# First chunk's first-layer up-products in two float32r parts, with a fourth buffer for converted weights

## The chip, the cores and the metric

The kernel runs on one core of one Trainium2 chip. The metric is the device time of one execution in microseconds (us); less is better. The engines are TensorE (PE: matrix products; PEld is its weight loads), VectorE (DVE), ScalarE (ACT), GpSimd (POOL) and SyncE (SP, which here only issues DMAs).

## The reference

Three layers follow each other in float32: attention that keeps the 32 largest scores of each row, and two pairs of dense products with 1152 tokens, width 512 and inner width 2048.

```python
def _attn_ref(q, k, v):                      # (2, 8, 576, 64) each
    scores = scale * np.matmul(q, k.transpose(0, 1, 3, 2))
    kth = np.partition(scores, -top_k, axis=-1)[..., -top_k:-top_k + 1]
    scores = np.where(scores >= kth, scores, -1000000000.0)
    scores = scores - np.max(scores, axis=-1, keepdims=True)
    attn = np.exp(scores)
    attn = attn / (np.sum(attn, axis=-1, keepdims=True) + 1e-09)
    return np.matmul(attn, v)

def _moe_ref(x, w_in, w_out):                # first layer
    h = x @ w_in
    return (np.maximum(h, 0.0) + np.log1p(np.exp(-np.abs(h)))) @ w_out

def _moe2_ref(x, w_in, w_out, alpha):        # second layer
    h = x @ w_in
    return (np.maximum(h, 0.0) + alpha * np.minimum(h, 0.0)) @ w_out
```

The weights reach the chip as float64 bit patterns; the kernel converts them to float32 itself.

## The kernel before

**Tiles and chunks.** The 1152 tokens are nine tiles of 128, in three chunks: tiles 3 and 4 (chunk 0), tiles 5, 6, 7 (chunk 1), tiles 8, 0, 1, 2 (chunk 2). A chunk's attention has to be done before its first layer, that before its second. The attention of the next chunk runs beside the layers of the one before.

**Attention.** A tile has eight heads, here called rows; row 76 is tile 7, head 6. For each row PE makes the scores (`pss`, L444), ACT copies them (`s`), DVE finds the 32 largest with four MAX8 and three MATCH_REPLACE8 (`m`, `r`, L453 and L456), a mask is built on ACT (L490) or DVE (L492), POOL subtracts it (`e`, L495), ACT takes the exponential and its sum (L497), PE transposes (`pp`, `pq`) and multiplies with the values (`pav`, L540). When a tile's eight rows are done, `finish` spreads the reciprocal sums with PE (`pr`), ACT copies that (`xn`), and DVE multiplies it with `pav`. With one part that product is the layer's input `xh`; with two parts it is `xn` (L598), from which ACT casts `xh` (L599) and POOL or DVE subtracts to get `xl`.

**Layers.** A layer has 16 steps j. `up(j)` is four products of 128 x 128 weights with n columns (n is 256, 384, 512 in chunks 0, 1, 2) into `ph`; ACT and DVE make `g` of it; `down(j)` multiplies `g` into the accumulators `pa`. In `NATIVE` layers the products are whole float32 (L637 for up, L685 for down), which the profile records as two matmuls each. In the others, `three` (L607 to L609) makes three float32r products of a high and a low part. The names carry layer and chunk: `ph00`, `pa00` first layer of chunk 0, `ph10`, `pa10` its second layer, `ph01` first layer of chunk 1. Before the change both layers of chunk 0 are `NATIVE`.

**Weights.** `convert` brings a float64 unit from memory (`cr`), makes the float32 unit `cx` with two DVE operations (L328, L333), one of ACT (L335, 2.5 us) and four of POOL (L339), and stores it as `ws`. There are 32 units; the first 24 are converted ahead, the last 8 when chunk 0's second layer first uses them, straight from `cx`. `fetch` loads a stored unit into a ring of four (`w`); where the layer is not native, `divide` splits it there: a cast on ACT (L357) and two subtractions of 512 columns on POOL (L351) or DVE (L352).

**Order.** Each engine runs its instructions in the order in which they stand. That order is made at build time by `Planner`: operations with lengths and due times, taken one after another by engine. The due times come from the tables at the head of the kernel (`T0`, `PACE`, `ROWS_DUE`, `AHEAD` and others). SP alone issues all DMAs.

## Time and profile before

| | us |
|---|---|
| median of 3 runs (684.16 to 687.32) | 685.82 |
| the profiled execution | 685.44 |
| its span | 683.7 |
| PE busy | 620.0 (91%) |
| DVE busy | 544.3 (80%) |
| ACT busy | 489.1 (72%) |
| POOL busy | 354.0 (52%) |

The profile's page gives busy time over the whole span, and the span in 40 slices of 17.1 us with the busy share of each in tenths. Stages are told apart by the first product of each: in this execution `ph00` starts at 133.7 us, `ph10` at 219.6, `ph01` at 296.2 (296.5 in the chain), the second layer of chunk 1 at 406.3, chunk 2 at 496.3. Matmul durations in the timeline contain the pipeline's depth; what one costs in a dense row of them is the distance of their starts, which the chain of waits prints as their length.

### The profile page before, as it was taken

The page shows a single profiled execution, that of the slowest core. Times are in us where ns is not written, and L with a number is a line of the kernel's source. Part 1 is how long each engine was busy: PE and PEld are TensorE (multiplying, and loading weights), DVE is VectorE, ACT ScalarE, POOL GpSimd, SP SyncE. Part 2 cuts the span into 40 slices and gives each one's busy share as a digit, 9 for nine tenths or more (in the row PEclk, how much of TensorE's full clock was granted, in tenths as well). Part 3 has the DMA queues.
Part 4 walks back from the last instruction along what each step waited for, and adds up shares of the span by engine and source line. Part 5 has one row for each costly group of instructions (what it writes and reads, how often), then busy time and mean ns, then how long its engine had stood idle before and what let it go on. Part 6 is the DMA issues. An engine that isn't in the chain of part 4 may idle for free.

```text
span 683.7 us, 10246 instructions
## 1 busy us (share of the span) xinstructions
PE 620.0 (91%) x3432; PEld 462.6 (68%) x3432; DVE 544.3 (80%) x1028; ACT 489.1 (72%) x981; POOL 354.0 (52%) x386
## 2 busy tenths in 40 slices
PE   5556545699999999999999999999999999999997
PEld 3334423466666666568788778788888888788885
DVE  5999999999999998999989899989654544544442
ACT  4877867798889778988889888777676555534431
POOL 0776665656564579657878768688310112121120
PEclk9566755699999999999999999999999999999999
DMA  8767865677787766732332122113243231313121
GB/s 332 255 244 232 261 210 208 203 289 244 293 268 262 277 225 209 246 128 88 121 112 77 66 89 93 63 63 124 77 154 107 80 123 63 123 62 123 62 93 62
DMA packets 28276, 109.59 MB, mean 160 GB/s; under 512 B 3264, under 2 KB 3264, under 8 KB 24128
## 3 DMA queue, kind: packets, MB, share of 16 engines
q1 hardware_dynamic: 28224, 108.94, 46.2%
q8 instruction: 27, 0.44, 0.3%
q14 instruction: 25, 0.20, 0.1%
HBM read 89.79 MB, written 19.14 MB: 159 GB/s over the span
## 4 chain that ended last, share of the span: by engine, by line
PE 76%; DVE 14%; ACT 3%; DMA 2%; issue 2%; POOL 1%; SPq 0%; DVEq 0%; POOLq 0%
PE ph L607 8%; PE pa L607 8%; PE pa L685 8%; PE ph L637 8%; PE ph L609 8%; PE ph L608 8%; PE pa L609 8%; PE pa L608 8%; DVE m L453 6%; DVE r L456 5%; PE pss L444 5%; PE pp L511 4%; DMA cr<-in_w_dram 2%; DVE cr L333 2%; DVE cx L328 2%
## 5 line engine op out<-in xcount | busy, mean ns | idle before, releaser
L453 DVE MAX8 m<-r 128x8 f32<-128x576 f32 x216 | 156.1, 746 | 0.2
L495 POOL TENSOR_TENSOR e<-s,e 128x288 f32<-128x288 f32 x144 | 124.1, 877 | 59.2 <-ACT e L490 40.2
L339 POOL TENSOR_TENSOR cx<-cx,cr 128x256 int32<-128x256 int32 x128 | 96.6, 780 | 74.6 <-ACT cr L335 64.0
L351 POOL TENSOR_TENSOR w<-w 128x512 fp32r<-128x512 f32 x66 | 90.2, 1378 | 72.9 <-ACT w L357 66.4
L456 DVE MATCH_REPLACE8 r<-m,r 128x576 f32<-128x576 f32 x144 | 106.3, 740 | 0.0
L351 POOL TENSOR_TENSOR gl<-g,gh 128x384 fp32r<-128x384 f32 (+1 forms) x38 | 44.2, 1162 | 104.3 <-ACT gh L665 104.1
L335 ACT ACTIVATE cr<-cr 128x1024 int16<-128x1024 uint32 x32 | 80.1, 2503 | 12.5 <-DVE cr L333 12.3
L444 PE MATMUL pss<-ks,q 64*128 64x288 f32 x320 | 75.5, 538 | 14.5 <-ACT s L449 6.2
L511 PE MATMUL pp<-ident,e 128*128 128x128 f32 x288 | 48.5, 302 | 39.2 <-ACT e L497 28.8
L511 PEld LDWEIGHTS pp<-ident,e 128*128 128x128 f32 x288 | 36.8, 154 | 57.9 <-ACT e L497 35.6
L357 ACT CAST w<-w 128x1024 fp32r<-128x1024 f32 x64 | 66.9, 1045 | 8.8 <-DMA w<-ws 8.8
L607 PE MATMUL pa<-w,gh 128*128 128x512 f32 x160 | 65.7, 410 | 0.0
L444 PEld LDWEIGHTS pss<-ks,q 64*128 64x128 f32 x320 | 34.7, 224 | 44.7 <-issue 11.9
L352 DVE TENSOR_TENSOR w<-w 128x512 fp32r<-128x512 f32 x62 | 48.0, 809 | 20.7 <-ACT w L357 20.6
L608 PE MATMUL pa<-w,gl 128*128 128x512 f32 x160 | 63.3, 396 | 0.0
L609 PE MATMUL pa<-w,gh 128*128 128x512 f32 x160 | 63.2, 395 | 0.0
L449 ACT COPY s<-pss 128x288 f32<-128x288 f32 x144 | 51.9, 406 | 14.1 <-PE pss L444 13.7
L453 DVE MAX8 m<-s 128x8 f32<-128x576 f32 x72 | 53.4, 746 | 10.4 <-ACT s L449 10.3
L652 DVE SCALAR_TENSOR_TENSOR g<-ph,g 128x256 f32<-128x256 f32 (+2 forms) x48 | 26.5, 552 | 41.4 <-ACT g L651 38.3
L497 ACT ACTIVATE e<-e,nb 128x576 f32<-128x576 f32 x72 | 55.7, 775 | 5.0 <-POOL e L495 5.0
L656 ACT ACTIVATE g<-ph 128x256 f32<-128x256 f32 (+2 forms) x48 | 23.8, 495 | 44.3 <-PE ph L609 37.9
L658 DVE SCALAR_TENSOR_TENSOR g<-g,rest,ph 128x256 f32<-128x256 f32 (+2 forms) x48 | 29.3, 611 | 31.8 <-ACT g L656 30.8
(127 smaller groups left out, 1417.4 us busy)
## 6 DMA issues: line engine op xcount, KB each, us to landing
w<-ws SPq DMA_DIRECT2D x88, 512.0 KB, 3.2
cr<-in_w_dram SPq DMA_DIRECT2D x32, 1024.0 KB, 6.9
ws<-cx SPq DMA_DIRECT2D x32, 512.0 KB, 7.6
v<-in_v_dram SPq DMA_DIRECT2D x12, 320.0 KB, 8.5
ks<-in_k_dram SPq DMA_DIRECT2D x12, 288.0 KB, 5.5
q<-in_q_dram SPq DMA_DIRECT2D x10, 256.0 KB, 6.0
out_dram<-o SPq DMA_DIRECT2D x9, 256.0 KB, 2.0
al<-in_alpha_dram SPq DMA_DIRECT2D x1, 8.0 KB, 9.0
```

What stands on the lines that cost most here:

```text
L335: op("ACT", ACT_LOW, due, lambda: nc.scalar.activation(raw().bitcast(I16)[:, :, 2], low(), AF.Copy, scale=2.0 ** -29), reads=[f], writes=[ ...
L339: op("POOL", on_pool(cs.stop - cs.start), due, lambda cs=cs: nc.gpsimd.tensor_add(f().bitcast(I32)[:, cs], f().bitcast(I32)[:, cs], high() ...
L351: lambda cs=cs: nc.gpsimd.tensor_sub(lo()[:, cs], x()[:, cs], hi()[:, cs].bitcast(F32)),
L357: op("ACT", on_act(WIDE), due, lambda: nc.scalar.copy(w()[:, 0, :], x()), reads=reads, writes=[w])
L444: nc.tensor.matmul(pss[n](), qr()[n * D:(n + 1) * D, pair, :], ks()[n * D:(n + 1) * D, cs], start=j == 0, stop=j == len(qk) - 1)
L453: op("DVE", on_dve(n), due, lambda: nc.vector.max(out=out(), in_=x()), reads=reads, writes=writes)
L456: op("DVE", on_dve(n) + 0.067, due, lambda: nc.vector.match_replace(out=out(), in_to_replace=found(), in_values=x(), imm_value=LOWEST), re ...
L495: op("POOL", on_pool(HS), due - AHEAD["mask"][ci], lambda cs=cs: nc.gpsimd.tensor_sub(e()[:, cs], s()[:, cs], e()[:, cs]), reads=[s], writ ...
L511: nc.tensor.transpose(pp()[:, c * P:(c + 1) * P], e()[:, c0 + c * P:c0 + (c + 1) * P], ident)
L607: nc.tensor.matmul(acc, ah, b_l, start=first, stop=False)
L608: nc.tensor.matmul(acc, a_l, bh, start=False, stop=False)
L609: nc.tensor.matmul(acc, ah, bh, start=False, stop=last)
```

## The change

The entries of `NATIVE` now name the part of a layer: `up` and `down` of chunk 0's second layer and `down` of its first layer stay whole float32, the first layer's `up` does not. So chunk 0's input has a high and a low part, the eight first-layer up units are divided in the ring, and the up-products go through `three` with 256 columns. The input's buffers are named by the chunk's parity in place of two in turn. `CXB`, the buffers for converted units, goes from 3 to 4. The planner's tables have new numbers throughout (a line or two shown), and the last six rows of each chunk get a due time of their own (`TAIL`). Code below moves down by one or two lines.

```diff
-MASK_SPARE = [134483.1, 915.2, -1585.2]
-CXB = 3
+MASK_SPARE = [1237.6, 843.7, -1292.2]
+CXB = 4
...
-PACE = [1522.8, 891.5, 6605.4, 9176.3, 2106.0, 687.1]
+PACE = [1786.6, 161.6, 6140.8, 8035.3, 911.5, 7716.3]
...
-NATIVE = {(1, 0), (0, 0)}
+TAIL = 6
+NATIVE = {(1, 0, 'down'), (0, 0, 'down'), (1, 0, 'up')}
...
-        return a + (b - a) * (i - first_row[ci]) / (first_row[ci + 1] - first_row[ci])
+        due = a + (b - a) * (i - first_row[ci]) / (first_row[ci + 1] - first_row[ci])
+        return due - AHEAD["tail"][ci] * (i >= first_row[ci + 1] - TAIL)
...
-    def features(name, bufs, ci, layer):
+    def features(name, ci, layer):
+        tag = name + str(ci % 2) * (not layer)
         n = sum(len(CHUNKS[c]) for c in (among[ci] if layer else [ci])) * P
-        if (layer, ci) in NATIVE:
-            return (buf(name + "h", bufs, [P, KT, n], F32, f"{name}h{ci}"),)
-        return tuple(buf(name + g, bufs, [P, KT, n], F32R, f"{name}{g}{ci}") for g in "hl")
+        if (layer, ci, "up") in NATIVE:
+            return (buf(tag + "h", 1, [P, KT, n], F32, f"{name}h{ci}"),)
+        return tuple(buf(tag + g, 1, [P, KT, n], F32R, f"{name}{g}{ci}") for g in "hl")
...
-            self.native = (layer, ci) in NATIVE
-            self.passes = 4 if self.native else 3
+            self.native = {part: (layer, ci, part) in NATIVE for part in ("up", "down")}
+            self.passes = {part: 4 if native else 3 for part, native in self.native.items()}
...
-                        if self.native:
+                        if self.native["up"]:
                             nc.tensor.matmul(hp(), whole_of(w)[:, cs], self.x[c][0]()[:, c, :],
...
-                        fetch((layer, (j + ULEAD) // GROUP, 0), no, ci, moe_due(ci, layer, j + ULEAD), lay.native)
+                        fetch((layer, (j + ULEAD) // GROUP, 0), no, ci, moe_due(ci, layer, j + ULEAD), lay.native["up"])
```

Three places of the new order follow; numbers behind a name tell buffers apart.

On PE, where the first layer of chunk 0 begins. `pp50`, `pp51`, `pq51` are transposes of tile 5's rows, `pr4` belongs to tile 4's finish. Before:

```order
L511 MATMUL pp50_1093<-ident_64,e0_71 128x128 x4
L587 MATMUL pr4__1103<-ident_64,rs4_961 64x128 x8
L511 MATMUL pp51_1116<-ident_64,e0_71 128x128 x4
L517 MATMUL pq51_1127<-ident_64,e0_71 128x128
L637 MATMUL ph00_0_1133<-xh0_628,w0_287 128x256 x4
L444 MATMUL pss560_1150<-ks13_620,q5_0_696 128x288
```

After:

```order
L589 MATMUL pr4__1104<-ident_64,rs4_1000 64x128 x8
L512 MATMUL pp51_1118<-ident_64,e0_71 128x128 x4
L518 MATMUL pq51_1134<-ident_64,e0_71 128x128
L445 MATMUL pss560_1139<-ks13_583,q5_0_691 128x288
L445 MATMUL pss570_1141<-ks13_583,q5_0_691 128x288
L541 MATMUL pav5__1147<-pt0_73,v10_139 64x128 x10
L445 MATMUL pss561_1179<-ks13_583,q5_0_691 128x288
L445 MATMUL pss571_1181<-ks13_583,q5_0_691 128x288
L609 MATMUL ph00_0_1189<-xl0_737,w0_287 128x256
L610 MATMUL ph00_0_1189<-xh0_712,w0_287 128x256
L611 MATMUL ph00_0_1189<-xh0_712,w0_287 128x256
```

Four score products and one value group of tile 5 now stand ahead of the first up-product, and where one whole product stood there are three.

On DVE, at the last MAX8 of tile 7 (row 76), the last tile of chunk 1; `cx107`, `cx116` are converted units, `g10_12` a step of chunk 0's second layer. Before:

```order
L453 MAX m77_2337<-r77_2353 128x8
L456 MATCH_REPLACE r76_2347<-m76_2325,r76_2347 128x576
L328 TENSOR_SCALAR cx107_2460<-cr107_2399 128x1024
L453 MAX m76_2325<-r76_2347 128x8
L333 TENSOR_SCALAR cr107_2399<-cr107_2399 128x1024
```

After:

```order
L454 MAX m81_2612<-s81_2536 128x8
L457 MATCH_REPLACE r76_2544<-m76_2470,r76_2544 128x576
L660 SCALAR_TENSOR_TENSOR g10_12_2614<-g10_12_2614,rest_70,ph10_12_2582 128x256
L329 TENSOR_SCALAR cx116_2631<-cr116_2570 128x1024
L454 MAX m76_2470<-r76_2544 128x8
```

One more unit is converted ahead of tile 7's last MAX8 than before, and the first MAX8 of rows 80 and 81 (chunk 2) both stand ahead of it.

On PE, from tile 7's `pr7` to the first product of chunk 1. Before:

```order
L587 MATMUL pr7__2606<-ident_64,rs7_2566 64x128 x8
L637 MATMUL ph10_15_2619<-yh0_1922,cx107_2460 128x256 x2
L685 MATMUL pa100_2007<-cx116_2521,g10_12_2430 128x512
L685 MATMUL pa101_2016<-cx116_2521,g10_12_2430 128x512
L637 MATMUL ph10_15_2619<-yh0_1922,cx107_2460 128x256 x2
L685 MATMUL pa100_2007<-cx116_2521,g10_13_2509 128x512
L685 MATMUL pa101_2016<-cx116_2521,g10_13_2509 128x512
L511 MATMUL pp81_2652<-ident_64,e0_71 128x128 x4
L517 MATMUL pq81_2657<-ident_64,e0_71 128x128
L607 MATMUL ph01_0_2661<-xl1_1674,w64_2165 128x384
```

After:

```order
L589 MATMUL pr7__2789<-ident_64,rs7_2711 64x128 x8
L687 MATMUL pa100_2133<-cx117_2718,g10_14_2698 128x512
L512 MATMUL pp80_2810<-ident_64,e0_71 128x128 x4
L687 MATMUL pa100_2133<-cx117_2718,g10_15_2748 128x512
L687 MATMUL pa101_2138<-cx117_2718,g10_14_2698 128x512
L687 MATMUL pa101_2138<-cx117_2718,g10_15_2748 128x512
L609 MATMUL ph01_0_2830<-xl1_1775,w64_2328 128x384
```

The last four `pa` products of chunk 0's second layer (steps 14 and 15), which stood behind the first products of chunk 1, now stand ahead of them.

## Rows read from the trace of the kernel before

**Rows 1.** The page's slices: busy tenths of PE, PE's clock.

```profile
PE   5556545699999999999999999999999999999997
PEclk9566755699999999999999999999999999999999
```

**Rows 2.** Busy by stage (windows): PE, PEld, DVE, ACT, POOL, clock, DMA share, GB/s.

```profile
0.00:133.70 133.70, 76.28 (x473) 50.32 (x473) 123.63 (x241) 94.68 (x185) 78.49 (x102) 0.66 0.72 244
133.70:219.60 85.90, 84.52 (x466) 54.50 (x466) 83.87 (x167) 76.27 (x166) 47.30 (x59) 1.00 0.78 277
219.60:296.20 76.60, 75.88 (x411) 49.67 (x410) 71.55 (x140) 62.75 (x124) 53.35 (x63) 1.00 0.65 221
296.20:406.30 110.10, 110.04 (x712) 85.94 (x710) 101.54 (x210) 96.41 (x227) 82.57 (x83) 1.00 0.30 101
```

**Rows 3.** PE's longest wait from 133.7 us on: us, times, longest.

```profile
PE pss L444 <- ACT pt L514: 1.4, 2, 0.9
```

**Rows 4.** Chain of waits around chunk 1's first product: start, us, what.

```profile
275.51 0.68 DVE m L453
...
282.70 0.67 PE pp L511 x4
...
289.57 1.02 PE pr__2606 L587 x16
...
296.50 0.18 PE ph L607
...
299.45 0.17 PE ph L609
```

**Rows 5.** Chain of waits in chunk 0's first layer: start, us, what.

```profile
154.96 1.73 PE ph L637 x8
156.68 1.72 PE pa L685 x4
...
166.21 0.69 PE pss L444 x4
166.90 1.24 PE pav__1378 L540 x20
```

**Rows 6.** Timeline of PE in chunk 2: start, us, instruction.

```profile
519.64 0.40 PE L608 MATMUL pa<-gh,w 128*128 128x512 f32 x1
...
529.91 0.39 PE L607 MATMUL ph<-xl,w 128*128 128x512 f32 x1
```

**Rows 7.** DVE by shape, 133.7 to 296.2 us: busy us, mean ns, idle before, releaser.

```profile
L453 DVE MAX8 m<-s 128x8 f32<-128x576 f32 x22 | 16.3, 750 | 3.3 <-ACT s L449 3.3
L333 DVE TENSOR_SCALAR cr<-cr 128x1024 uint32<-128x1024 uint32 x17 | 14.1, 832 | 0.0
L328 DVE TENSOR_SCALAR cx<-cr 128x1024 uint32<-128x1024 uint32 x17 | 13.9, 816 | 1.0 <-DMA cr<-in_w_dram 0.7 <-PE ph L637 0.3
...
L658 DVE SCALAR_TENSOR_TENSOR g<-g,rest,ph 128x256 f32<-128x256 f32 x16 | 7.6, 476 | 2.0 <-ACT g L656 1.9
...
L352 DVE TENSOR_TENSOR w<-w 128x512 fp32r<-128x512 f32 x2 | 2.3, 1162 | 0.0
...
L352 DVE TENSOR_TENSOR xl<-xn,xh 128x256 fp32r<-128x256 f32 x2 | 1.7, 836 | 0.1
L492 DVE TENSOR_SCALAR e<-s,m 128x576 f32<-128x576 f32 x2 | 1.2, 602 | 0.0
```

**Rows 8.** ACT by shape in the same stretch.

```profile
L335 ACT ACTIVATE cr<-cr 128x1024 int16<-128x1024 uint32 x18 | 45.2, 2513 | 0.5 <-DVE cr L333 0.3
...
L357 ACT CAST w<-w 128x1024 fp32r<-128x1024 f32 x4 | 4.2, 1048 | 0.0
...
L599 ACT CAST xh<-xn 128x512 fp32r<-128x512 f32 x3 | 1.8, 616 | 1.6 <-DVE xn L598 1.6
```

**Rows 9.** POOL by shape in the same stretch.

```profile
L351 POOL TENSOR_TENSOR w<-w 128x512 fp32r<-128x512 f32 x6 | 8.4, 1412 | 0.7 <-ACT w L357 0.6
```

**Rows 10.** The first DVE operation of a conversion: duration ns, min/median/max.

```profile
L328 DVE TENSOR_SCALAR cx<-cr x32: 642/692/1265, 12.0 to 291.4; 128x1024 uint32<-128x1024 uint32 x32
```

More of the change, by code (lines that the diff above doesn't have):

```diff
@@ L37 @@
 LOADER = 'SP'
-STORER = 'SP'
+STORER = "SP"
 ISSUE = {"SP": 0.45, "ACT": 0.45, "POOL": 1.0}
@@ L48 @@
 VB = 5
-XB = 2
 XNB = 1
 OB = 4
-SPARE = [-863.9, 913.9, 6123.9]
-MASK_SPARE = [134483.1, 915.2, -1585.2]
-CXB = 3
+SPARE = [100.9, 5669.5, 14147.0]
+MASK_SPARE = [1237.6, 843.7, -1292.2]
+CXB = 4
 LEAD = 4
@@ L58 @@
 ACT_LOW = 2.26
-T0 = 477.6
+T0 = 1940.7
 VALUES = 1.35
 SCORES = 0.69
-PACE = [1522.8, 891.5, 6605.4, 9176.3, 2106.0, 687.1]
-ROWS_DUE = [(-1662.9, -1003.4), (1658.6, 430.2), (497.6, 12385.0)]
-EARLY_DUE = [-2024.4, -649.3, 3228.3]
-LOAD_LEAD = 54844.0
-FETCH_LEAD = [425.2, -1254.7, -724.3]
+PACE = [1786.6, 161.6, 6140.8, 8035.3, 911.5, 7716.3]
+ROWS_DUE = [(-1939.3, -998.3), (968.4, 370.7), (1235.3, 13006.5)]
+EARLY_DUE = [-2598.1, -150.5, 113.2]
+LOAD_LEAD = 2030105.1
+FETCH_LEAD = [-4094.2, 1312.8, -118897.9]
 EARLY = 24
-DIRECT_LEAD = 2317.1
-RAW_LEAD = 38707.1
-AHEAD = {'scores': [1150.5, 2758.1, 5135.1], 'mask': [162.1, -369.7, 1298.4], 'flip': [1999.5, 1156.6, 5731.8], 'values': [-8975.3, 471.5, -4037.1], 'chain': [238970.7, 5908.4, -285.0], 'split': [-1840.8, -579.3, 257.9], 'edge': [10354.4, -910.2, 4322.8]}
+DIRECT_LEAD = 111332.4
+RAW_LEAD = 1513453.1
+AHEAD = {'scores': [43150.3, 254.7, 234.3], 'mask': [-521.3, -2026.0, 588.8], 'flip': [-222.9, 8785.2, 8396.0], 'values': [-2594.2, 4709.7, -4575.5], 'chain': [223075.3, 3031.3, -1669.3], 'split': [-952.3, -3341.7, 6180.2], 'edge': [2701.0, -150.1, 5445.2], 'tail': [-2829.4, 883.1, -466.2]}
+TAIL = 6
 MASKS = [['act'], ['act'], ['act']]
-NATIVE = {(1, 0), (0, 0)}
+NATIVE = {(1, 0, 'down'), (0, 0, 'down'), (1, 0, 'up')}
 WINDOW = 3.41333
@@ L573, in finish @@
         if ti == 0:
-            xs[ci] = features("x", XB, ci, 0)
+            xs[ci] = features("x", ci, 0)
         av, total = tiles[t]["av"], tiles[t]["sum"]
@@ L619, in __init__ @@
             self.x = [xs[ci]] * KT if layer == 0 else ys.pop(ci)
-            self.native = (layer, ci) in NATIVE
-            self.passes = 4 if self.native else 3
-            self.turned = layer == 0 and ci == len(CHUNKS) - 1 and len(among[ci]) == 1 and not self.native
+            self.native = {part: (layer, ci, part) in NATIVE for part in ("up", "down")}
+            self.passes = {part: 4 if native else 3 for part, native in self.native.items()}
+            self.turned = layer == 0 and ci == len(CHUNKS) - 1 and len(among[ci]) == 1 and not self.native["down"]
             self.g = {}
@@ L642, in products @@
                                   c == 0, c == KT - 1)
-                op("PE", self.passes * step * (max(n, 134) / 2390 if self.native else max(n, 260) / 2195), due, products,
+                op("PE", self.passes["up"] * step * (max(n, 134) / 2390 if self.native["up"] else max(n, 260) / 2195), due, products,
                    reads=[w] + [x for c in range(c0, c0 + step) for x in self.x[c][-2:]], writes=[hp])
@@ L659, in up @@
                     g(), g(), rest[:, j:j + 1], hp(), op0=ALU.mult, op1=ALU.add), reads=[hp, "rest"], writes=[g])
-            if self.native:
+            if self.native["down"]:
                 self.g[j] = (g,)
@@ L683, in products @@
                 def products(acc=acc, cs=cs):
-                    if self.native:
+                    if self.native["down"]:
                         nc.tensor.matmul(acc(), gh()[:, cs], whole_of(w)[:, w0:w0 + DM], start=first, stop=last)
@@ L694, in down @@
                 due = moe_due(ci, self.layer, min(j, FJ - 2) + ULEAD) + (0.01 * i if j >= FJ - 2 else 0.0)
-                op("PE", self.passes * (self.n if self.turned else DM) / (2390 if self.native else 2195), due, products,
+                op("PE", self.passes["down"] * (self.n if self.turned else DM) / (2390 if self.native["down"] else 2195), due, products,
                    reads=[*parts_of_g, w], writes=[acc])
@@ L712, in down @@
             if self.layer == 0 and not before:
-                ys[group[-1]] = [features("y", 1, group[-1], 1)] * KT
+                ys[group[-1]] = [features("y", group[-1], 1)] * KT
             os = [buf("row", OB, [P, DM], F32, f"o{nm}{ti}") for ti in range(len(self.tiles))]
@@ L770, in topk_attention_moe_kernel @@
                     if j % GROUP == 0:
-                        fetch((layer, j // GROUP, 1), no, ci, moe_due(ci, layer, j + ULEAD), lay.native)
+                        fetch((layer, j // GROUP, 1), no, ci, moe_due(ci, layer, j + ULEAD), lay.native["down"])
                     lay.down(j)
```

## The prediction

> **What bounds the kernel now.** I read the slices first, to find the stages, then the windows by stage, then who waits for whom in each, and last the chain of waits where one chunk gives way to the next. The slices [rows 1] show PE at half load for eight slices and full from there to the end. Up to 133.7 us, DVE is the busy engine, 123.6 us of it, while PE's clock is at 0.66 of full in the mean [rows 2]. From `ph00` at 133.7 us on PE hardly stops, at full clock; its longest wait, 1.4 us in all, is in [rows 3]. So at first sight every microsecond taken from PE's products after 133.7 us comes off the end.
>
> The second sight is in the stage from `ph00` to `ph01` (133.7 to 296.2 us). PE is busy 160.4 of 162.5 us there, but DVE 155.4 and ACT 139.0 [rows 2]. Both are close to full at once. What DVE does there is above all chunk 1's attention, without which `ph01` can't begin. The chain of waits shows the tie: tile 7's last MAX8 ends at 276.2 us, its transposes run on PE at 282.7, its `pr` at 289.6, the first product of chunk 1 at 296.5 [rows 4]: 20.3 us from DVE's last word on chunk 1 to its use. In those 20 us PE is kept busy with the rest of chunk 0's second layer. DVE after `ph01` has room (101.5 of 110.1 us), PE has none.
>
> **The up-products.** A whole float32 product of 256 columns is two records, eight records are 1.73 us, so 0.4325 us [rows 5]. There are 4 x 16 = 64: 27.7 us. They become 192 float32r products of 256 columns, a shape the trace lacks. The nearest rows: 384 columns take 3.12 us / 18 = 0.173 us (the 18 records from 296.50 to 299.62 us) [rows 4]; 512 columns take 10.27 us / 44 = 0.2334 us between starts [rows 6]. Per column that is 0.451 and 0.456 ns: in proportion, with no fixed part to be seen. So 256 columns: 0.117 us, three 0.350, 64 x 3 = 22.4 us, a saving of 5.3 us. The upper bound is a product as dear as at 384 columns: 3 x 0.173 = 0.520 us, 5.6 us lost instead. A gain beyond the columns' share has no row for it. I take 0.117, since two lengths lie on one line.
>
> A rule of the Trainium skill speaks against that: TensorE: Matmul & The Clock Gate, section LDWEIGHTS, gives a load of 128 columns as 128 / 1.2 = 107 ns, and its Part 3 says that loads overlap running products only where the row groups differ. By that page three loads and three streams would be an estimated 0.64 us in place of 0.43 us, some 13 us lost. The trace disagrees: at 384 columns nothing of a load shows in the gap. Whether a load hides behind 256 columns too no row here shows.
>
> **What the two parts cost elsewhere.** Eight weight casts on ACT at 1.05 us, 8.4 us; two input casts at 0.62 [rows 8]. Sixteen subtractions of 512 columns, all on POOL by the new order, at 1.41 us [rows 9], 22.6 us; three of the units are divided before `ph00`, where ACT is busy 94.7 of 133.7 us and POOL 78.5, and cost nothing there. The other five lie after it: 5.2 us of ACT, 14.1 us of POOL, which has 100.7 of 162.5 us taken [rows 2]. SP issues as many DMAs as before in nearly the same order. On the way to the first product tile 4's input now needs a cast (0.62) and a subtraction (0.84, [rows 7]) more, with the hand-over about 1.6 us: `ph00` at about 135.3.
>
> **The moves.** I counted the two orders by the prices of [rows 5]. Ahead of `ph00` PE gets four score products (1.4 us) and ten value products (1.2) more, 2.6 us; these go into time in which PE waits anyway. From `ph00` to `ph01` PE's sum falls by 4.9 us: the up-products' 5.3 and the attention moved ahead come off, and the last four `pa` products of chunk 0's second layer (4 x 0.43 x 2 = 3.4 us), which stood after `ph01`, come in. Behind `ph01` PE has 2.9 us less, those 3.4 less half a microsecond of attention, with as many changes between attention and layer products (40 groups of attention work there in either order).
>
> **What sets `ph01`.** Take PE first: it needed 162.5 us less its 2 us of waits, so 160.4; less 4.9 is 155.5, and from 135.3 it would reach `ph01` at 290.8. Then DVE: up to tile 7's last MAX8 the new order adds a MAX8 (0.75), a conversion's two operations (0.82 + 0.83), two masks (1.2) and an `xl` (0.84), and takes two `w` subtractions away (2.3) [rows 7]: 4.4 - 2.3 = 2.1 us more. With DVE 96% busy in that stage that moves the last MAX8 from 276.2 to 278.3. The 20.3 us behind it stay: from the first transpose to `ph01` the new order has about as much on PE, and the ACT conversion ahead of the exponentials is there in both. So `ph01` comes at about 298.6, some 8 us after PE could have begun it. **PE's saving is turned into PE's waiting.** What is left of it at the end is what was moved out from behind `ph01`.
>
> **The sum**, from the profiled execution's 685.44 us (0.4 below the median): + 2.1 (DVE ahead of chunk 1) - 2.9 (less behind `ph01`) = 684.6. One thing works the other way. DVE lost 3.3 us to score copies and 1.9 to second-layer copies in that stage [rows 7], both behind products of PE, which now runs ahead; 5.2 us is the most that this gives, 0 the least. In the head, where PE also runs ahead, DVE idles 10.1 of 133.7 us, the start included [rows 2], so some must go; I take 1 us. The fourth `cx` buffer frees at most the 1.0 us that conversions waited, for DMA mostly; I take nothing. **Forecast: 683.6 us.**
>
> POOL's added work may also cost DVE something: the first operation of a conversion runs from 642 to 1265 ns, 692 in the median [rows 10], 816 in the mean of this stage [rows 7], with POOL busy 62% of it. With 14.1 us more on POOL, a seventh, the excess of 174 ns grows by 25 ns, over some 35 operations 0.9 us; I leave it in the range. The Trainium skill has the cause in SBUF — State Buffer, section Who interferes with whom: VectorE and GpSimd share a pair of ports under an exclusive lock; by it single conversions could stretch to the 1265 ns seen, and the spread of that row agrees.
>
> **The rivals.**
> 1. *The saving comes through.* DVE's waits on PE's products vanish altogether: 684.6 - 5.2 = 679.4. For it: PE is ahead by 8 us. Against: the score copies are queued on ACT, which has more to do. PE's own limit, `ph01` at 290.8, would be 7.8 us under the sum, 676.8; only with less DVE work is that reached.
> 2. *ACT becomes the bound, and it ends slower.* From tile 4's `xn` to `ph01` ACT has five casts more (5 x 1.05 = 5.2 us; a few small copies and one conversion fewer, 2.5 us, about even out). ACT is at 76.3 of 85.9 us in chunk 0's first layer [rows 2], and its queue is in order: score copies, masks and exponentials of chunk 1 stand behind the casts. If they can't be fitted into its gaps, `ph01` comes 5.2 us later still: 684.6 + 5.2 = 689.8. It decides once ACT has less than 5 us of usable gaps of the 23.5 it had in 162.5 us. Against: that is four times as much.
> 3. *256 columns are as dear as 384.* Then up-products cost 33.2 us and not 22.4, 10.8 more. The 8 us in which PE would wait take most: 2.8 us are left, 684.6 + 2.8 = 687.4. For it: three loads in place of two. Against: the straight line of the two lengths.
>
> **How the numbers follow.** What a measurement can tell from no change is about 0.5%, 3.4 us: 682.4 to 689.2. The forecast gets 0.50, with its own range from 681 to 686; the saving through 0.28; ACT 0.13; dear columns 0.06; anything else, above all waits behind `ph01`, where PE lost a spare 3.4 us of chunk 0's work, 0.03. Faster by over 0.5%: the 0.28 and a low corner of the forecast, 0.33. Slower: most of ACT's and a part of the last two, 0.14. Within: 0.53. The range reaches from the first rival to the second: 679.0 to 690.0.
>
> **What would show it.** Right: up-products at L609 to L611 0.117 us apart; PE with several microseconds of waits between `ph00` and `ph01`, on transposes that wait for ACT or POOL, and chunk 1's first product at 297 to 299 us; 384 us from there to the span's end. The first rival: that product before 294 us. The second: ACT near 95% there and DVE waiting for `s`. The third: 0.17 us apart. Wrong altogether: PE waiting a few microseconds behind `ph01`, or the head longer than 135 us by more than one.

## The result, and the profile after

The changed kernel takes 693.34 us in the median (692.53 to 699.01, 4 runs) against 685.67 of the kernel before on the same chip: a ratio of 1.012, with a 95% interval from 1.009 to 1.015. It is slower by more than the half per cent that the chances were drawn for, and outside the range. The profiled execution took 693.58 us, its span is 690.9 (683.7 before).

The page's slices of the kernel after, busy tenths of PE and PE's clock, as [rows 1]:

```profile
PE   4576844699798999999999999999999999999997
PEclk9555555699999999999999999999999999999999
```

The stages of the kernel after (windows: length, busy PE, PEld, DVE, ACT, POOL, clock, DMA share, GB/s), to be read against [rows 2]; they end at the first product of `ph00`, `ph10`, `ph01` and at the span's end:

```profile
0.00:141.26 141.26, 86.90 (x501) 56.60 (x501) 127.39 (x246) 104.36 (x196) 89.68 (x114) 0.61 0.70 236
141.26:223.11 81.85, 73.32 (x463) 48.85 (x462) 77.39 (x153) 71.44 (x146) 62.73 (x70) 1.00 0.85 290
223.11:306.31 83.20, 82.42 (x455) 52.99 (x455) 79.57 (x155) 67.38 (x141) 56.64 (x67) 1.00 0.59 201
306.31:690.90 384.59, 380.54 (x2082) 307.22 (x2080) 262.90 (x472) 254.28 (x513) 172.61 (x161) 1.00 0.27 93
```

The kernel before has, for the same stages, 133.7, 85.9, 76.6 and 387.5 us. So the head is 7.6 us longer, chunk 0's first layer 4.1 shorter, its second 6.6 longer, the rest 2.9 shorter. For the last stage of the kernel before, which [rows 2] does not have as a whole:

```profile
296.25:683.70 387.45, 383.31 (x2086) 308.09 (x2084) 265.23 (x483) 255.31 (x510) 174.85 (x162) 1.00 0.27 94
```

PE's work behind `ph00` did fall, from 543.7 to 536.3 us. But it fell by 11.2 us in chunk 0's first layer (84.5 to 73.3), where PE then waits 8.5 us, and grew by 3.8 behind `ph10` (459.2 to 463.0), where PE hardly waits. So `ph10` comes 3.5 us later than before, and from there to the end it takes 3.7 us more: together the 7.2 us between the spans. PE's waits from `ph00` to `ph10` in the kernel after (total, times, longest):

```profile
PE ph L609 <- DVE g L654: 2.0, 2, 1.6
PE pr__1687 L589 <- ACT s L450: 1.7, 1, 1.7
PE ph L639 <- ACT yh L568: 1.6, 1, 1.6
PE pa L687 <- DMA w<-ws: 1.6, 1, 1.6
PE pp L512 <- ACT e L498: 1.4, 2, 1.1
```

Before, the largest group of PE's waits from `ph00` on was the 1.4 us of [rows 3]. The up-products themselves did what was said of them. The timeline of PE at the first of them (start, us, instruction):

```profile
141.48 0.29 PE L610 MATMUL ph<-xh,w 128*128 128x256 f32 x1
141.61 0.28 PE L611 MATMUL ph<-xh,w 128*128 128x256 f32 x1
141.73 0.28 PE L609 MATMUL ph<-xl,w 128*128 128x256 f32 x1
141.85 0.28 PE L610 MATMUL ph<-xh,w 128*128 128x256 f32 x1
```

They start 0.12 us apart, three in 0.36 us, where one whole product took 0.43 [rows 5].

The clearest difference is in the chain of waits through the head. The summary line of that chain from 28 us to `ph00`, first of the kernel before, then of the kernel after:

```profile
by line: DVE m L453 28.1%; DVE r L456 23.5%; issue 9.8%; DVE cr L333 9.6%; DMA cr<-in_w_dram 8.1%; DVE cx L328 7.4%; POOL cx L339 4.6%; POOL e L495 2.9%; ACT cr L335 2.4%; PE pr__1103 L587 1.8%; PE pp L511 1.0%; DVE xh L594 0.7%; ACT xn L59
```

```profile
by line: DMA cr<-in_w_dram 18.7%; POOL cx L340 14.3%; issue 14.0%; DVE m L454 13.0%; DVE r L457 11.9%; POOL e L496 7.0%; DVE cx L329 4.9%; ACT cr L336 4.4%; DVE cr L334 4.3%; POOL w L352 3.7%; POOL xl L352 1.6%; ACT e L491 0.7%; DVE rs L581
```

Before, the chain runs along DVE: MAX8, MATCH_REPLACE8 and the two operations of a conversion are two thirds of it, POOL's lines 7.5%. After, POOL's four lines are 27%, the loads of raw weights 19%, DVE a third. The head's pace has gone over from DVE to POOL and the ring of conversions, and POOL's new lines (`w`, `xl`) are in the chain.

### The profile page after: what moved, and what is told of

Its sections match the earlier page's. It is cut to its first block, busy times and chain, and to the rows that moved or that the text cites. A ratio compares the mean times of both kernels' runs of the same rounds, so it can differ in the third digit from the quotient of the medians.

```text
span 690.9 us, 10432 instructions
## 1 busy us (share of the span) xinstructions
PE 623.2 (90%) x3496; PEld 465.7 (67%) x3496; DVE 547.3 (79%) x1023; ACT 497.5 (72%) x993; POOL 381.7 (55%) x410
## 4 chain that ended last, share of the span: by engine, by line
PE 70%; DVE 11%; POOL 6%; DMA 6%; ACT 4%; issue 3%; SPq 0%; POOLq 0%; DVEq 0%
PE ph L609 9%; PE ph L610 8%; PE ph L611 8%; PE pa L609 8%; PE pa L610 7%; PE pa L611 7%; PE pa L687 6%; DMA cr<-in_w_dram 5%; PE ph L639 4%; PE pss L445 4%; DVE m L454 4%; DVE r L457 3%; POOL cx L340 3%; PE pp L512 3%; ACT cr L336 2%
## 5 line engine op out<-in xcount | busy, mean ns | idle before, releaser
L352 POOL TENSOR_TENSOR w<-w 128x512 fp32r<-128x512 f32 x84 | 116.4, 1398 | 72.7 <-ACT w L358 67.7
L496 POOL TENSOR_TENSOR e<-s,e 128x288 f32<-128x288 f32 x144 | 121.2, 855 | 43.5 <-ACT e L491 28.3
L340 POOL TENSOR_TENSOR cx<-cx,cr 128x256 int32<-128x256 int32 x128 | 99.3, 798 | 64.3 <-ACT cr L336 59.8
L352 POOL TENSOR_TENSOR gl<-g,gh 128x384 fp32r<-128x384 f32 (+1 forms) x37 | 42.4, 1145 | 105.2 <-ACT gh L667 105.0
L445 PE MATMUL pss<-ks,q 64*128 64x288 f32 x320 | 78.4, 553 | 16.8 <-ACT s L450 10.4
L358 ACT CAST w<-w 128x1024 fp32r<-128x1024 f32 x72 | 75.3, 1045 | 8.3 <-DMA w<-ws 8.2
L512 PE MATMUL pp<-ident,e 128*128 128x128 f32 x288 | 50.1, 309 | 30.8 <-ACT e L498 18.3
L609 PE MATMUL ph<-xl,w 128*128 128x256 f32 (+2 forms) x192 | 69.5, 362 | 2.0 <-DVE g L654 2.0
L610 PE MATMUL ph<-xh,w 128*128 128x256 f32 (+2 forms) x192 | 64.7, 337 | 0.0
L611 PE MATMUL ph<-xh,w 128*128 128x256 f32 (+2 forms) x192 | 64.6, 336 | 0.0
L353 DVE TENSOR_TENSOR w<-w 128x512 fp32r<-128x512 f32 x60 | 46.4, 809 | 20.8 <-ACT w L358 20.7
```

What stands on the lines that cost most here:

```text
L340: op("POOL", on_pool(cs.stop - cs.start), due, lambda cs=cs: nc.gpsimd.tensor_add(f().bitcast(I32)[:, cs], f().bitcast(I32)[:, cs], high() ...
L352: lambda cs=cs: nc.gpsimd.tensor_sub(lo()[:, cs], x()[:, cs], hi()[:, cs].bitcast(F32)),
L358: op("ACT", on_act(WIDE), due, lambda: nc.scalar.copy(w()[:, 0, :], x()), reads=reads, writes=[w])
L445: nc.tensor.matmul(pss[n](), qr()[n * D:(n + 1) * D, pair, :], ks()[n * D:(n + 1) * D, cs], start=j == 0, stop=j == len(qk) - 1)
L496: op("POOL", on_pool(HS), due - AHEAD["mask"][ci], lambda cs=cs: nc.gpsimd.tensor_sub(e()[:, cs], s()[:, cs], e()[:, cs]), reads=[s], writ ...
L512: nc.tensor.transpose(pp()[:, c * P:(c + 1) * P], e()[:, c0 + c * P:c0 + (c + 1) * P], ident)
```

## The experiments

Four theories were told apart. **A**: the head is longer because of where instructions stand in the new order. **B** (called P once POOL was suspected): it is longer because the division's own work, on POOL above all, holds up what DVE needs. **C**, the prediction's: DVE's work bounds chunk 1's start, and PE's saving becomes waiting. And its rival: PE is the bound from `ph00` on. In the runs e1 to e4 and e9 to e15 the order of one of the two kernels is kept instruction by instruction, and only what is named is moved, added or left out; in e5 to e8 the planner makes its own order.

All of them in one table. The stages are those of each run's profiled execution, which need not be the median one (e15's is its fastest of 12); the last column is the time up to `ph10` in which DVE was not busy, from the windows. The kernel before had medians of 685.7 to 687.0 beside them.

| run | median us | ratio (95%) | head | to `ph10` | to `ph01` | rest | DVE idle |
|---|---|---|---|---|---|---|---|
| before | 685.7 | | 133.7 | 85.9 | 76.6 | 387.5 | 12.1 |
| after | 693.3 | 1.012 (1.009 to 1.015) | 141.3 | 81.9 | 83.2 | 384.6 | 18.3 |
| e1 | 703.8 | 1.025 (1.022 to 1.028) | 138.3 | 94.4 | 83.2 | 384.6 | 27.6 |
| e2 | 695.8 | 1.014 (1.012 to 1.017) | 142.6 | 83.8 | 83.2 | 384.6 | 18.4 |
| e3 | 698.9 | 1.019 (1.016 to 1.022) | 134.0 | 95.2 | 83.2 | 384.6 | 21.2 |
| e4 | 691.5 | 1.007 (1.005 to 1.010) | 137.8 | 84.4 | 83.8 | 384.8 | 18.8 |
| e5 | 710.6 | 1.035 (1.032 to 1.038) | 137.1 | 87.0 | 99.4 | 383.1 | 14.1 |
| e6 | 695.6 | 1.013 (1.011 to 1.015) | 136.0 | 86.7 | 86.6 | 384.7 | 14.9 |
| e7 | 704.1 | 1.026 (1.023 to 1.029) | 140.6 | 85.7 | 91.4 | 383.8 | 18.8 |
| e8 | 702.0 | 1.022 (1.020 to 1.024) | 135.0 | 86.7 | 95.1 | 383.3 | 13.9 |
| e9 | 704.1 | 1.026 (1.023 to 1.029) | 143.1 | 95.1 | 77.1 | 387.4 | 29.3 |
| e10 | 705.4 | 1.029 (1.025 to 1.032) | 143.6 | 94.2 | 78.7 | 387.3 | 33.0 |
| e11 | 700.5 | 1.021 (1.016 to 1.025) | 136.3 | 96.2 | 78.5 | 387.3 | 25.1 |
| e12 | 690.5 | 1.007 (1.004 to 1.011) | 136.3 | 86.9 | 76.6 | 387.3 | 16.4 |
| e13 | 692.7 | 1.008 (1.005 to 1.011) | 136.5 | 85.0 | 83.2 | 384.6 | 18.3 |
| e14 | 697.7 | 1.016 (1.013 to 1.019) | 142.4 | 85.0 | 83.2 | 384.6 | 15.9 |
| e15 | 685.7 | 1.000 (0.997 to 1.003) | 132.5 | 83.9 | 77.8 | 387.4 | 10.7 |

### Moving what stands ahead of the first product (e1, e2, e3)

The tail of the head in the kernel after, from its timeline, rows between them left out:

```profile
128.75 1.09 PE L589 MATMUL pr__1104<-ident,rs 128*64 128x128 f32 x16
...
131.92 2.48 ACT L336 ACTIVATE cr<-cr 128x1024 int16<-128x1024 uint32 x1
...
134.72 0.58 ACT L593 COPY xn<-pr__1104 128x512 f32<-128x512 f32 x1
...
136.39 0.62 ACT L601 CAST xh<-xn 128x512 fp32r<-128x512 f32 x1 [0.26 <-DVE xn L600]
...
137.44 2.40 PE L541 MATMUL pav__1147<-pt,v 128*64 128x128 f32 x20
137.51 0.74 POOL L352 TENSOR_TENSOR xl<-xn,xh 128x256 fp32r<-128x256 f32 x1
...
138.94 0.40 DVE L353 TENSOR_TENSOR xl<-xn,xh 128x256 fp32r<-128x256 f32 x1
...
141.26 0.39 PE L609 MATMUL ph<-xl,w 128*128 128x256 f32 x1
```

Tile 4's `pr` is done at 129.8 us, but ACT copies it only at 134.7, behind a conversion; and when the low part is complete, at 139.3, PE is still at tile 5's products, at half clock, until 141.3. Both look like repairable faults of the order. The numbers in the diffs are the planner's operations: 365 is the last `xl`, 1057 to 1064 are `ph00` steps 0 and 1, 598 and 618 tile 5's scores and values, 360 to 364 tile 4's `pr`, `xn`, multiply, `xh` and first `xl`, 643 the bias of row 54.

```diff
-        for i, way in plan.order():
+        for i, way in place(plan.order(), 365, [1057, 1058, 1063, 1064, 598, 618]):
```

> The order of after, with one place changed: tile 5's four score products and ten value products, which stood between the last transposes of row 51 and the first up-product, stand behind the first two steps of up-products. In the profile of after those products run from 135.8 to 141.3 us at half clock, and the last half of the input's low part is done at 139.3. Theory A (the head got longer because of what stands in the queues between tile 4's pr and ph00, this being one of two such places): ph00 at 139.4 instead of 141.3; as the moved 2.6 us come back behind it, the total goes by -1.9 to +0.7 us, 691.4 to 694.0. Rival B (the head is longer because of the division's own work): ph00 stays above 140.5.

`ph00` came at 138.3, and the time rose to 703.8. The windows of e1 and its row of waits (PE from 150 to 175 us) tell why:

```profile
138.27:150.00 11.73, 8.44 (x52) 7.07 (x52) 6.61 (x15) 5.64 (x13) 5.53 (x8) 0.74 0.51 156
```

```profile
PE ph L609 <- DVE g L654: 4.4, 1, 4.4
```

PE stood still before `ph00` (2.5 us for `xl`), the first products ran at half clock (mean 0.74 up to 150 us, 0.21 us apart in place of 0.12), and the third step then waited 4.4 us for DVE's `g`, which stands in DVE's queue behind attention. That attention was itself waiting for the scores that this edit had put off. The waits of DVE and ACT in e1 from 138 to 152 us:

```profile
DVE m L454 <- ACT s L450: 5.1, 1, 5.1
```

```profile
ACT s L450 <- PE pss L445: 5.3, 1, 5.3
```

So e1 does not test an earlier `ph00` alone. In the kernel after PE was busy 5.9 of the last 6.3 us ahead of `ph00`, and the clock is 1.00 from there on.

```diff
+    order = place(order, 593, [360, 361, 362, 355, 363, 364, 643])
+    order = place(order, 657, [365])
```

> The order of after, with tile 4's finish moved forward in the queues: on ACT the copy of pr (xn) and the cast xh stand ahead of the bias of row 54 and of the conversion's 2.5 us, on DVE the multiply stands ahead of the conversion's second operation, on POOL the subtraction ahead of the conversion's additions. Nothing is left out. Theory A: pr at 128.8 as before, xn at 130.5, the low part done by 134; then PE still has tile 5's products in front, about 5.5 us at half clock, so ph00 at 138.5 to 139, total about 691. Rival B: ph00 stays above 140.5, since the extra cast and subtraction are the same.

The low part was complete at 134.3 as expected, but `ph00` came at 142.6, later than in the kernel after: the transposes' copy `pt`, now behind the same conversion on ACT, is what PE waits for next (3.1 us, from 133.1 to 136.2), and tile 5's products follow it.

Both together, with `ph00` behind 597, the last transpose's copy, in place of 365:

> Both moves together: tile 4's finish first in the queues, and tile 5's products behind the first two steps of up-products. Theory A: ph00 at 133.5 to 135, as the prediction had it, 6 to 7.5 us earlier than in after. What reaches the end: if PE is the bound from ph00 on, the head's gain less the 2.6 us of products that are now behind, total 688 to 690; if the waits in chunk 0's first layer (8 us in after) take the moved products, 686 to 687. Rival B: ph00 above 139, total above 692. Rival C (DVE bounds chunk 1's start, as the prediction said): ph00 earlier, but ph01 within 1 us of after's 306.9 and the total within 1 us.

`ph00` at 134.0, where theory A wanted it, and the total at 698.9: all of it and more was given back in the next stage, 95.2 us long in place of 81.9, with 4.9 us of PE waiting for the first `g` on DVE and the clock at 0.71 up to 150 us. Here DVE did not idle; from `ph00` to 150 us it was busy 15.9 of 16.0 us:

```profile
133.96:150.00 16.04, 11.16 (x66) 10.02 (x67) 15.90 (x34) 11.98 (x25) 9.63 (x12) 0.71 0.65 193
```

**An earlier `ph00` is worth nothing by itself**; DVE's queue and the conversions in it have not moved. In all three, as in the kernel after, what follows `ph10` takes 83.2 and 384.6 us to within 0.1: with this order PE sets the pace there, and everything is decided ahead of `ph10`.

### Undoing parts (e4 to e8)

```diff
-                        if self.native["up"]:
+                        if self.native["up"] or self.ci == 0:
```

(and no casts and subtractions for chunk 0's input and up-weights, at their places in the order of after)

> The order of after, word for word, with the split undone in it: chunk 0's up-products are whole float32 again, and the casts and subtractions of its input and of its up-weights are gone from the places in which they stood; all else, the fourth buffer too, as in after. Theory A (order): ph00 at 138 to 140.5, since the copy of tile 4's pr stands behind a conversion on ACT all the same, and the score and value products still stand in front; the up-products cost 5.3 us more on PE behind it; total 693 to 697. Rival B (the division's own work): ph00 at 133 to 135 and the total at 688 to 691.

The time is 691.5: undoing the whole split gives back some 2 of 7.7 us. The head falls by 3.5 us, and of the 5.3 us that the products take longer 2.6 show in the first layer. The order of after is thus some 5 us slower than that of before even without the split.

```diff
-CXB = 4
+CXB = 3
```

(e7 has this line alone, e5 all planner tables of before besides; e6 keeps `CXB = 4` and has `(0, 0, 'up')` back in `NATIVE`; e8 is the kernel before with `CXB = 4`)

> The split alone: up-products in two parts with all that they need, but the planner's tables and the three buffers of before. So far, undoing the split inside the order of after gave back 2 us of 7.7. Theory A (the new tables' order, not the split, makes the head longer): ph00 at 134 to 138, total 684 to 689. Rival B (the split's own work makes the head longer): ph00 at 139 or more, total above 691.

> The tables and the fourth buffer alone: chunk 0's up-products stay whole float32, the planner makes its own order from the numbers of after. Theory A: the head stays longer than that of before, ph00 at 136 to 140, total 689 to 695. Rival B: ph00 at 133 to 135, total 683 to 687.

> After with three buffers for converted units in place of four, the order made anew by the planner from the same numbers. In after DVE waits 7.1 us for raw units from memory up to tile 7's last MAX8, 1.8 in before. If the fourth buffer lets conversions run into memory's limit, those waits fall under 4 us and the total to 688 to 691; if the fourth buffer bears on nothing, the total stays within 2 us of 693.3; if the tables need it, it goes above 696.

> Before with four buffers for converted units, all else the same, the order made anew. The prediction gave the fourth buffer nothing, at most 1.0 us of gain. Right if the total lies within 684 to 688; if the buffer by itself disturbs the order, it lies above 689.

All four are slower than before, at 695.6 to 710.6 us; the new tables without the split (e6) are no faster than the kernel after. Of the single parts they tell little: each makes the planner build another order, and most of the loss lies from `ph10` to `ph01` (86.6 to 99.4 us), far from what was edited. By these runs the tables of each kernel fit its own operations and buffers and no others. That is why the next runs keep an order and put things into it.

### The split in the order of before (e9 to e12, e15)

e9 has before's order on DVE and SP and, but for what is added, on the others. The casts and subtractions go in where what they need is ready.

```diff
+        start[i] = max(end[b] for b in plan.ops[i][1]) + 0.3
...
-                nc.tensor.matmul(hp(), whole_of(w)[:, cs], self.x[c][0]()[:, c, :],
+                three(hp(), w()[:, 0, cs], w()[:, 1, cs], xh()[:, c, :], xl()[:, c, :],
```

> The split alone, in the order of before word for word on all five engines (DVE, SP and the rest of ACT, POOL and PE stand as in before, three buffers for converted units), with the casts and subtractions put in as soon as what they need is there, all subtractions on POOL. This takes the planner out of the question. The prediction's steps, without its moves: ph00 at 135.3 (1.6 us later than 133.7), 5.3 us less on PE behind it, waits of PE that take part of that back; total 682 to 686. Theory A (order alone made the head longer): as the prediction. Rival B (the division's work holds up conversions and masks on POOL, which hold up DVE): ph00 at 138 or later, PE waits of 5 us or more behind it, total above 689.

In this order rival B is right: `ph00` at 143.1, 704.1 us. A piece of e9's timeline shows how (rows between left out):

```profile
58.90 1.26 POOL L353 TENSOR_TENSOR w<-w 128x512 fp32r<-128x512 f32 x1
...
60.14 2.56 POOL L341 TENSOR_TENSOR cx<-cx,cr 128x256 int32<-128x256 int32 x3
...
62.66 1.53 POOL L499 TENSOR_TENSOR e<-s,e 128x288 f32<-128x288 f32 x2
64.23 0.77 ACT L501 ACTIVATE e<-e,nb 128x576 f32<-128x576 f32 x1 [4.19 <-POOL e L499]
65.12 0.17 DVE L584 TENSOR_SCALAR rs<-sum 128x8 f32<-128x8 f32 x1 [2.35 <-ACT e L501]
```

A weight's subtraction stands ahead of a conversion's additions, these ahead of a mask; ACT waits 4.2 us for the mask, and DVE 2.4 us for ACT's sums. POOL's share of the chain (28 us to `ph00`) is 46.6 us here, against 8.0 before and 30.2 in the kernel after. Its summary line has the weights' subtractions (`POOL w`); none of their casts is in the chain:

```profile
by line: issue 22.8%; POOL cx L341 19.9%; POOL e L499 14.5%; DVE m L457 10.7%; DVE r L460 7.8%; DMA cr<-in_w_dram 5.2%; ACT cr L337 4.3%; POOL w L353 4.0%; DVE cr L335 2.2%; POOL xl L353 2.1%; DVE cx L330 1.6%; ACT pt L518 1.0%; PE pp L515 
```

e10 keeps all of that and leaves out the gain: each up-product is one whole float32 product again, of the weight's second part with one part of the input.

```diff
-                            three(hp(), w()[:, 0, cs], w()[:, 1, cs], xh()[:, c, :], xl()[:, c, :],
+                            nc.tensor.matmul(hp(), w()[:, 1, cs].bitcast(F32), (xl if c < KT // 2 else xh)()[:, c, :].bitcast(F32),
```

> The same, but the up-products are whole float32 products as in before (two records in place of three) and read one part of weight and input alone; so the division's casts and subtractions stay and the products' saving is left out. Against e9 it costs 5.3 us more if PE bounds all that lies behind ph00, and 0 to 2 us if e9 loses the saving in waits. Against before it shows what the added work by itself costs: 1.6 to 3 us by theory A, 6 us or more by rival B.

705.4 us: the products' 5.3 us are worth 1.3 us here, less than the two intervals can tell apart. The division alone costs 18.7. Its parts, taken away one by one (`LEAVE` units, 3 or 8, are not divided; cast and subtractions go together):

```diff
+LEAVE = 3
...
-            divide(ci, w, x, due - AHEAD["split"][ci], due, [], (layer, ci) == (0, 0))
+            divide(ci, w, x, due - AHEAD["split"][ci], due, [], (layer, ci) == (0, 0), (layer, ci) == (0, 0) and j < LEAVE)
```

> e10 (the order of before, whole float32 up-products, the division as dead work) with the division of the first three up-units left out: three casts on ACT and six subtractions on POOL, all ahead of ph00. Theory P (the subtractions stand in POOL's queue ahead of the conversions' additions and of the masks, and so make POOL the end of the head's chain): ph00 from 143.6 back to 136 to 138, since 6 x 1.27 = 7.6 us of POOL are gone; total 705.4 down to 697 to 700. Rival I (the input's own cast and low part do it, at tile 3 and 4): ph00 stays above 141, total above 702.

> e10 with the division of all eight up-units left out, so that only the input's casts and low parts remain as added work. Theory P: besides the head, chunk 0's first layer goes from 94.2 us back to 86 to 88, as ten subtractions (14 us of POOL) are gone there; total 688 to 691. Rival I: ph00 above 141 and the total above 700. If only the head falls and the layer stays at 94, then it is the late start and the low part of the input that make the layer long, and the total is 696 to 700.

The windows of head and first layer, in the order e10, e11, e12:

```profile
0.00:143.60 143.60, 74.15 (x474) 50.30 (x474) 127.22 (x248) 101.37 (x194) 89.03 (x112) 0.77 0.68 232
143.60:237.83 94.23, 89.45 (x467) 56.88 (x467) 77.61 (x154) 75.72 (x165) 59.33 (x70) 0.95 0.71 239
```

```profile
0.00:136.29 136.29, 74.99 (x474) 49.81 (x474) 127.32 (x248) 99.11 (x191) 79.84 (x106) 0.74 0.71 244
136.29:232.45 96.16, 89.55 (x466) 56.92 (x467) 80.03 (x154) 75.91 (x165) 60.16 (x70) 0.94 0.69 236
```

```profile
0.00:136.34 136.34, 74.92 (x474) 49.75 (x474) 127.21 (x249) 99.12 (x191) 79.80 (x106) 0.69 0.71 244
136.34:223.26 86.92, 85.91 (x466) 55.47 (x467) 79.66 (x160) 72.55 (x161) 47.52 (x60) 0.98 0.77 266
```

The three units ahead of `ph00` are worth 7.3 us of head (143.6 to 136.3), nearly the 7.6 us (6 x 1.27) that their subtractions take on POOL, although POOL is busy only 89 of 143.6 us. The five later ones are worth 9.2 us of the first layer (96.2 to 86.9). The input's two parts that remain cost 2.6 us at `ph00`. In totals: 4.9, 10.0 and 4.3 us (690.5 less 686.2).

e15 is the counterpart, the gain without any of the cost: the three products of each place all read the undivided weight and input, and every division is left out.

```diff
-                            nc.tensor.matmul(hp(), whole_of(w)[:, cs], self.x[c][0]()[:, c, :],
+                            three(hp(), w()[:, 1, cs], w()[:, 1, cs], x, x, c == 0, c == KT - 1)
```

> The order of before, word for word, with chunk 0's first-layer up-products as three float32r products of 256 columns and nothing added anywhere: they read the undivided input and weight three times. So the products' saving of 5.3 us comes free, and every division is left out. If DVE and what feeds it set the pace up to chunk 0's second layer (theory of the prediction's second sight): PE waits 4 to 5 us more there, ph10 within 1 us of 219.6, total 685 to 687. If PE is the bound from ph00 on: ph10 at 214 to 215, total 680 to 682; then the whole question is the price of the division. In between: the share of the 5.3 us that a version with a cheaper division could win at most.

The ratio is 1.000 (0.997 to 1.003). Its windows of chunk 0's two layers, to be read against [rows 2]:

```profile
132.49:216.43 83.94, 81.05 (x531) 54.36 (x531) 82.16 (x163) 75.26 (x165) 47.50 (x59) 1.00 0.81 281
216.43:294.19 77.76, 76.11 (x413) 49.72 (x411) 73.83 (x144) 63.75 (x124) 53.71 (x63) 1.00 0.65 221
```

PE is busy 3.5 us less in the first layer, which is 2.0 us shorter, and waits 2.9 us in it (1.4 before); the next stage is 1.2 us longer. `ph10` came at 216.4, so "within 1 us of 219.6" was missed; 1.2 of the 3.2 us are the head's. **Even for nothing, the shorter products bring nothing that can be measured**, at most 0.3% by the interval. Ahead of `ph10` PE alone is not the bound.

### The division in the order of after (e13, e14)

```diff
-            divide(ci, w, x, due - AHEAD["split"][ci], due, [])
+            divide(ci, w, x, due - AHEAD["split"][ci], due, [], ci == 0)
```

(and the three products read the undivided weight three times)

> The order of after, word for word, with the division of all eight up-units left out (eight casts, sixteen subtractions); the up-products stay three float32r products of 256 columns, but all three read the undivided weight. So the products' saving and the input's two parts stay, and the weights' division costs nothing. Theory P (the division of the weights is what after pays for): ph00 from 141.3 to 136 to 138.5, PE's waits between ph00 and chunk 0's second layer from 8.5 to 3 to 6 us, total 684 to 688, within half a percent of before or under it. Rival O (the new order itself is longer, with or without the division): ph00 at 140 or later, total above 690.

Half of theory P: the head falls by 4.8 us to 136.5, and its chain goes back to DVE (66.6 us of it from 28 us on, POOL 11.2; 39.9 and 30.2 in the kernel after). But the first layer grows by 3.1 us, PE waiting 4.4 us for ACT's score copies at tile 5's `pr`, and the total is 692.7, 0.7 below the kernel after. By the ratios to the kernel before, 1.008 and 1.012, it is some 2.6 us, and their intervals overlap. In the order of after the division of the weights costs little in the end: rival O holds for the total, not for `ph00`.

```diff
+    order = [(i, 1 if i in (1055, 1056, 1071, 1072, 1092, 1093) else way) for i, way in order]
```

> After, with the six subtractions of the three units that are divided ahead of ph00 moved from POOL to DVE, at the same places of the order. Theory P (it is POOL's queue): the head's chain leaves POOL, but DVE, busy 127 of 141 us, takes six times 0.6 to 1.2 us instead; ph00 at 138 to 141, total 690 to 693. If the place does not matter and only the amount of work does: ph00 and total as in after, within 1 us. If DVE has no room at all: ph00 at 143 or later, total above 695.

697.7 us: POOL leaves the chain, DVE is busy 131.9 us in the head in place of 127.4, and it ends at 142.4. Neither engine has room for these six operations.

## Why the prediction was wrong, step by step

**The price of the products: right.** 0.12 us apart against 0.117 forecast. The rule of the Trainium skill that was weighed against it (TensorE: Matmul & The Clock Gate, section LDWEIGHTS with Part 3) does not hold here: the loads take 0.19 us each in the trace, one for each product, and none of it shows between products that start 0.12 us apart. Dear columns (rival 3) are out.

**PE's saving turned into PE's waiting: right, but not at the place named.** From `ph00` to `ph01` PE waits 9.3 us in the kernel after and 2.1 before. e15 shows it without anything else: of 3.2 us less work in that stretch, 2.4 became waits. The saving that comes through (rival 1) is out for the same reason.

**From DVE's last MAX8 to `ph01`, and from there to the end: the lengths right, the tie not.** Two rows of after, from DVE's timeline and the chain, answer [rows 4]:

```profile
286.35 0.74 DVE L454 MAX8 m<-r 128x8 f32<-128x576 f32 x1
```

```profile
306.87 0.18 PE ph L609
```

That is 19.8 us after the last MAX8 (20.3 forecast), and 384.0 us before the end (384). But in the kernel before, DVE's last MAX8 is in the chain to `ph01` [rows 4]; in the kernel after the chain from 270 to 312 us is PE's own work, with no row of DVE:

```profile
by line: PE pa L687 34.1%; PE ph L639 25.1%; PE pss L445 11.6%; PE pav__2397 L541 8.9%; PE pp L512 6.2%; PE ph L609 3.8%; PE ph L610 2.9%; PE ph L611 2.9%; PE pr__2789 L589 2.6%; ACT s L450 1.6%; PE pq L518 0.8%; issue 0.1%
```

PE is busy 82.4 of the 83.2 us from `ph10` to `ph01`. So `ph01` was late because `ph10` was late and PE had more to do behind it, not because PE waited there for chunk 1. That the distance of 20 us came out all the same was luck, as far as the reason given goes.

**"Cost nothing there": the step that failed.** The three units divided ahead of `ph00` were put into the idle time of ACT (94.7 of 133.7 us busy) and POOL (78.5). In the order of before they cost 7.3 us of head (e10, e11); in the order of after, leaving out the weights' division takes 4.8 us off it (e13). The share of busy time said that there was room. It did not say that POOL, which waited 31 us for ACT's half of the conversions in the head of before, stands in the middle of two chains (raw unit, `cx`, the next raw unit; mask, exponential, sums, `xn`), so that what is put ahead of their pieces delays them:

```profile
L339 POOL TENSOR_TENSOR cx<-cx,cr 128x256 int32<-128x256 int32 x56 | 42.5, 780 | 35.9 <-ACT cr L335 31.3 <-PE pss L444 4.6
```

The five later units were let pass with "100.7 of 162.5 us taken" by the same reasoning; they cost 9.2 us (e11, e12). Rival 2 was the right kind of rival on the wrong engine: it asked for ACT's gaps and priced 5.2 us, and the chains of e9 and of the kernel after go over POOL. No run leaves out the casts on ACT without the subtractions, so the share of the casts rests on these chains alone.

**`ph00` at 135.3: 6.0 us off.** The input's own part was 1.6 us in the sum and is 2.6 in e12. Between single profiles a microsecond is not told apart (last section). The rest came in the order of after by delays along DVE: DVE's waits up to tile 7's last MAX8, in the kernel before (up to 276.2 us) and after (up to 287.1):

```profile
DVE cx L328 <- DMA cr<-in_w_dram: 1.8, 3, 0.7
...
DVE xh L594 <- PE pav__312 L540: 0.9, 1, 0.9
```

```profile
DVE cx L329 <- DMA cr<-in_w_dram: 7.1, 8, 1.3
DVE xn L600 <- PE pav__317 L541: 4.0, 1, 4.0
```

**DVE's sum, + 2.1 us: it was 10.9** (last MAX8 ended at 287.1, not 276.2). It counted DVE's work and took 1 us off its waits. By the windows DVE was busy 265.3 us up to there (259.5 before) and idle 21.8 (16.7): 5.8 and 5.1 us more. Of the 5.8, most is in one group of DVE's operations by shape, before and after:

```profile
L328 DVE TENSOR_SCALAR cx<-cr 128x1024 uint32<-128x1024 uint32 x30 | 24.0, 800 | 2.3 <-DMA cr<-in_w_dram 1.8 <-PE ph L637 0.3
```

```profile
L329 DVE TENSOR_SCALAR cx<-cr 128x1024 uint32<-128x1024 uint32 x31 | 29.3, 946 | 7.2 <-DMA cr<-in_w_dram 7.1
```

One operation more (0.8, forecast), and 146 ns more for each of 31, 4.5 us. The prediction left 25 ns, 0.9 us, in the range, scaled from POOL's busy share. Up to `ph10` the operation takes 821 ns before, 899 after and 826 in e13 (25 of them each): there the weights' subtractions on POOL are nearly all of the growth, 2 us. The six behind `ph10` take the other 2.6; from 223 to 306 us the mean is 759 ns before, 1076 after and 1026 in e4, which has no division in chunk 0, so that part belongs to the new order. The Trainium skill, SBUF — State Buffer, section Who interferes with whom, has the two engines share a pair of ports under an exclusive lock. The trace agrees in so far as the operation grows by 73 ns with POOL's subtractions beside it; that the lock is the cause no run here shows.

**The moves.** "Time in which PE waits anyway" was right of the four score and ten value products in so far as they cost nothing that e1 could win back: with them behind `ph00` ACT and DVE go without scores for 5 us, and the kernel is 10 us slower. The 8 us that PE was to wait ahead of `ph01` are there (8.5 up to `ph10`, 0.8 behind), but as a string of short waits on DVE, ACT and a weight's load, not one wait for chunk 1. What the sum from `ph00` to `ph01` did not show is that the new order also moves PE's work inside that stretch: `pa` products and attention of chunk 1, 6.5 us in all, come in between `ph10` and `ph01`, where PE has no time to spare, and only 2.8 us leave the stage behind it.

**The fourth buffer: not settled.** Nothing was given for it. Each kernel becomes 11 to 15 us slower with the other's number (e7, e8), but by another order, not by waits for a buffer that the runs could show.

So the 10.0 us between 683.6 and the profiled 693.6 are: 6.0 at `ph00`; 2.3 from there to `ph01` (165.6 us by the chain, 163.3 forecast); 1 for waits of DVE that did not go; 0.9 of the execution outside the span (2.7 in place of 1.7 us); and 0.3 less in the last stage. The cause, as far as the runs go: the division costs 15 us for the weights and 4 for the input where the old order stands (e10 to e12), the saving is worth nothing measurable (e15), and the new tables make room for the division at the price of an order that is some 5 us slower without it (e4). Most of that price can be placed: from `ph10` to the end all runs in the order of after take 467.8 to 468.6 us, those in the order of before 463.9 to 466.0, and PE is busy nearly throughout. What else the order costs ahead of `ph10` stays open: moves at its most suspicious place (e1 to e3) made it worse. DVE's idle time up to `ph10` goes with it: 18.3 to 18.8 us in after, e4 and e13, with or without a division, 12.1 before.

## What to carry to other kernels

Before adding work to an engine with idle time, look at what that engine's idle time waits for and at who waits for it: POOL was busy 59% of the head, and 7.6 us more work there came out as 7.3 us. Price a saving on the stage's bound, and try it free of its costs first, as e15 does: in the old order that one run shows that there is nothing to pay for. Where tables have been fitted to a kernel's order, test parts in a kept order; a newly made one differed by more (9 to 24 us here) than the part is worth. And when an order moves work, ask on which side of a wait it lands: what was moved behind `ph10` here was paid in full.

## What the hardware showed beyond that

- In e1 PE waited 2.5 us ahead of `ph00`, and the 24 products that follow start 0.21 us apart, not 0.12, with 0.74 of the clock granted up to 150 us; in the kernel after, with PE busy up to `ph00`, they start at full clock. By the distances of their starts that is some 2 us for the 24 products; the larger loss of e1 is the wait for scores.
- Up to `ph00` before and e15 are the same program, but it came at 133.7 and 132.5 us, with a mean clock of 0.66 and 0.74: single profiles of such a head differ by a microsecond.
